# Attention and an expert layer on one core: the order of all operations laid out anew, with the filling matmuls placed again

## The chip, the core and the metric

The kernel runs on one core of one Trainium2 chip. The metric is device time in microseconds (us), median of the runs. A core has TensorE (PE: matmuls and transposes, with weight loads shown as PEld), VectorE (DVE), ScalarE (ACT), GpSimd (POOL) and SyncE (SP), each with its own queue of instructions that it works off in order. They wait for one another through semaphores.

## The reference, cut to what matters

Inputs are q, k and v of shape (4, 8, 768, 64): batches, heads, positions, width. A chunk is 32 positions of k; each query keeps the 6 chunks with the highest upper bound, and only those behind it.

```python
ub = sum(maximum(q * k_min, q * k_max), axis=-1)      # k_min, k_max per chunk of 32
ub = where(causal, ub, -1e9); top_chunks = argsort(ub)[..., -6:]
scores = where(chunk is in top_chunks and pos_q >= pos_k, q @ k.T / 8, -1e9)
attn = softmax(scores) @ v                             # (4, 8, 768, 64)
x = attn as (3072, 512)
h = x @ w_in                                           # (512, 2048)
out = softplus(h) @ w_out                              # (2048, 512)
```

## The kernel before

The work is cut into 12 blocks of 256 queries (4 batches of 3 blocks, all 8 heads at once as 4 pairs). For each block n the stages are:

- loads of q, k and v (`ld`), and transposes: blocks 0 to 2 on PE (`kT`, `qT`, L480), later ones by DMA from SP's queue (`kD`, `qD`);
- largest and smallest key of each chunk on DVE (`kx`, `kn`, L499 and L507), copies of these into a block-diagonal tile BD (`bd`), copies of K and of q into their places (`kc`, `qac`), positive and negative parts of q (`qpn`);
- the bounds on PE (`ub`, L579 and L583), on DVE the causal addition (`uba`), the sixth largest (`mx`, L606) and the mask (`raw`, L621 and L624, tile `mraw`), its transpose (`mT` on PE for blocks 0 to 2, L636 and L642; `mD` by DMA later) and the copies of the mask beside q (`mc`), so that the scores' matmul adds it;
- scores (`s`, L696 and L697, two matmuls each), exponential on ScalarE (`ex`, L704), the causal cut on GpSimd (`af`, L714), times v (`av`, L726), division on DVE (`nm`, L739 and L740), transpose into x (`oT` and `xc` in blocks 0 to 2 and 11, `xD` by DMA otherwise);
- the expert layer: `h` on PE (L895), exponential and logarithm on ScalarE (`e` L900, `ln` L905), the second matmul `y`. Blocks 4 to 10 make it of seven half-size products (L840) with differences on DVE (`dl`, `dh`, `dd`, `de`, `df`) and sums of the weights (`wd`, `wh`, `wv`); the others plainly (L925). The epilogue's small operations are `yr`, `yz`, `yv`, `yc`, `yd`, `ye`, `yw`, `yx`, `yf`, and `st` stores.

Nothing of this is in program order. `make_plan` makes operations with their dependencies, and the string `ORDER` lists all of them in one sequence: a letter for the engine (P, A, V, G, S), the name and, with #, which of that name (without #, the next one not yet placed). `in_order` hands out buffers in that sequence, and each engine's instructions are issued in it; a semaphore is all that holds an instruction back at run time. Many operations may run on either of two engines, and the letter chooses.

A word `z` with a number is no work of the plan: it makes matmuls on a tile of zeros, one of 512 columns (L1011) for every four and one of 128 columns (L1013) for each of the rest. They write a PSUM bank that the next real user clears.

```python
if word[0] == "z":
    order.append(int(word[1:]))
...
for _ in range(o // 4):
    nc.tensor.matmul(T.pools["y"].homes[0], T.zero, wide, start=True, stop=True)
for _ in range(o % 4):
    nc.tensor.matmul(T.pools["y"].homes[0][:, 0:128], T.zero, T.zero, start=True, stop=True)
```

Of the kernel before, what the change touches and what calls it, by code (L numbers as in the profile page):

```python
# [1047 lines left out]
```

## Time and profile before

| | |
|---|---|
| median of 3 runs | 256.06 us (256.02 to 256.46) |
| the profiled execution's own time | 256.22 us |
| its span, first to last instruction | 254.5 us |
| PE, ACT, DVE, POOL busy | 247.7, 212.2, 177.5, 119.6 us |
| matmuls | 2790, of them 86 on zeros |

The span is what the trace shows of one execution; what lies around it (256.22 less 254.5) is not seen in it. A matmul's row lasts longer than its place in the stream, as the next one starts before it ends: a PE that is shown busy can still have started its matmuls later than it could have. So the starts of matmuls are compared, beside the busy time.

### The profile page before, as it was taken

The page shows a single profiled execution, that of the slowest core. Times are in us where ns is not written, and L with a number is a line of the kernel's source. Part 1 is how long each engine was busy: PE and PEld are TensorE (multiplying, and loading weights), DVE is VectorE, ACT ScalarE, POOL GpSimd, SP SyncE. Part 2 cuts the span into 40 slices and gives each one's busy share as a digit, 9 for nine tenths or more (in the row PEclk, how much of TensorE's full clock was granted, in tenths as well). Part 3 has the DMA queues.
Part 4 walks back from the last instruction along what each step waited for, and adds up shares of the span by engine and source line. Part 5 has one row for each costly group of instructions (what it writes and reads, how often), then busy time and mean ns, then how long its engine had stood idle before and what let it go on. Part 6 is the DMA issues. An engine that isn't in the chain of part 4 may idle for free.

```text
span 254.5 us, 7076 instructions
## 1 busy us (share of the span) xinstructions
PE 247.7 (97%) x2790; PEld 202.7 (80%) x2790; DVE 177.5 (70%) x568; ACT 212.2 (83%) x389; POOL 119.6 (47%) x197
## 2 busy tenths in 40 slices
...
GB/s 170 147 133 129 193 195 193 162 164 152 138 130 145 188 157 135 142 172 194 159 146 158 100 119 168 43 24 36 8 85 62 3 206 3 1 85 3 0 58 193
DMA packets 113954, 29.90 MB, mean 117 GB/s; under 512 B 103776, under 2 KB 110944, under 8 KB 113920
## 3 DMA queue, kind: packets, MB, share of 16 engines
...
## 4 chain that ended last, share of the span: by engine, by line
PE 88%; DVE 8%; DMA 2%; issue 1%; ACT 0%; DVEq 0%
PE ph L895 31%; PE py L925 10%; PE pt L840 9%; PE py L840 8%; PE ps L696 6%; PE po L726 6%; PE ps L697 4%; PE py L1011 3%; DMA mT<-mraw 2%; PE ph L925 2%; PE pt L696 2%; DVE kx L507 2%; PE pt L726 2%; PE pt L579 2%; PE pt L697 1%; DVE qa L294 1%
## 5 line engine op out<-in xcount | busy, mean ns | idle before, releaser
L895 PE MATMUL ph<-x,w_in_sb 128*128 128x256 bf16 x768 | 97.9, 272 | 0.0
L704 ACT ACTIVATE pt<-ps 128x512 bf16<-128x512 f32 (+1 forms) x145 | 75.5, 550 | 9.3 <-PE ps L697 8.2
L714 POOL TENSOR_SCALAR_AFFINE_SELECT pt<-pt 128x256 bf16<-128x256 bf16 x96 | 40.7, 447 | 89.5 <-ACT pt L704 80.7
L895 PEld LDWEIGHTS <-w_in_sb 128*128 128x128 bf16 x768 | 72.4, 98 | 9.0
L900 ACT ACTIVATE e<-ph 128x512 f32<-128x512 f32 x96 | 57.0, 607 | 15.2 <-PE ph L895 15.0
L905 ACT ACTIVATE g<-e 128x1024 bf16<-128x1024 f32 x48 | 50.5, 1065 | 0.4
L925 PE MATMUL py<-w_out_sb,g 128*128 128x512 bf16 (+1 forms) x144 | 33.5, 367 | 0.0
L726 PEld LDWEIGHTS <-pt 128*128 128x128 bf16 x672 | 28.5, 97 | 2.6
L704 ACT ACTIVATE pt<-pt 128x512 bf16<-128x512 f32 (+1 forms) x47 | 26.3, 571 | 3.9 <-PE pt L697 3.1
L925 PEld LDWEIGHTS <-g 128*128 128x128 bf16 x176 | 16.4, 98 | 11.7
L726 PE MATMUL po<-v,pt 128*128 128x65 bf16 x516 | 24.4, 193 | 0.0
L840 PEld LDWEIGHTS <-g 128*128 128x128 bf16 x224 | 21.2, 98 | 2.6
L499 DVE TENSOR_REDUCE kx<-kT 128x32 bf16<-128x1024 bf16 x18 | 21.5, 1209 | 1.1 <-DMA kT<-io 1.0
L363 POOL DMA_DIRECT2D v<-in_v_dram x24 | 21.7, 908 | 0.0
L363 POOL DMA_DIRECT2D io<-in_k_dram x22 | 20.1, 921 | 0.0
L363 POOL DMA_DIRECT2D io<-in_q_dram x22 | 19.7, 901 | 0.1
L696 PE MATMUL ps<-qa,ka 96*128 96x256 bf16 x72 | 19.0, 273 | 0.7 <-DVE qa L294 0.6
L696 PE MATMUL ps<-qt,kb 128*128 128x256 bf16 x73 | 19.1, 272 | 0.0
L739 DVE RECIPROCAL rew<-po 128x4 f32<-128x4 f32 x38 | 6.7, 177 | 16.1 <-PE po L726 15.9
L840 PEld LDWEIGHTS <-df 128*128 128x128 bf16 x168 | 16.0, 98 | 2.0
L697 PE MATMUL ps<-qt,kb 128*128 128x256 bf16 (+1 forms) x73 | 17.3, 245 | 0.0
L740 DVE TENSOR_TENSOR osw<-po,rew 128x256 bf16<-128x256 f32 x38 | 16.1, 424 | 1.3
...
## 6 DMA issues: line engine op xcount, KB each, us to landing
out_dram<-ysb SPq DMA_DIRECT2D x23, 256.0 KB, 2.6
...
wx<-in_k_dram SPq DMA_DIRECT2D x2, 256.0 KB, 3.8
wx<-in_q_dram SPq DMA_DIRECT2D x2, 256.0 KB, 4.0
```

What stands on the lines that cost most here:

```text
L363: lambda e, t=t: nc.gpsimd.dma_start(out=into(nm, n, t), in_=rows(nm, n, t)),
L499: nc.vector.tensor_reduce(kx.ap[:, :, j].rearrange("d p (t c) -> d t p c", t=NT), kT.ap.rearrange("d p x -> d (p x)").rearrange("d (t p c ...
L696: nc.tensor.matmul(sp.ap[:, 0:QB], kk[0:nr, p, j * 128:(j + 1) * 128], qq, start=True, stop=True)
L697: nc.tensor.matmul(sp.ap[:, QB:w], kk[0:nr, p, (j + 1) * 128:(j + 2) * 128], qq[:, 1] if last else qq, start=True, stop=True)
L704: lambda e, sp=sp, pt=pt, h=h, j=j, w=w: nc.scalar.activation(pt.ap[:, h, j:j + 2].rearrange("k j c -> k (j c)")[:, 0:w], sp.ap[:, 0:w], A ...
L714: nc.gpsimd.affine_select(out=d, in_=d, compare_op=ALU.is_ge, fill=0.0, base=0, channel_multiplier=-1, pattern=[[0, 2], [1, 128]])
L726: nc.tensor.matmul(o[:, u, h], pt.ap[:, h, j, c0:c0 + 128], T.V[i][:, j, 2 * p + h, :], start=(j == 0), stop=(j == t0 + u))
L840: nc.tensor.matmul(bank.ap[:, c * HD:(c + 1) * HD], a(f), w(f), start=start and f == 0, stop=f == HF - 1, skip_group_check=True)
L895: nc.tensor.matmul(o[:, j], T.w_in[:, dt, ft * 128:(ft + 1) * 128], x.ap[:, dt], start=(dt == 0), stop=(dt == KDM - 1))
L900: lambda e, hb=hb, eb=eb, f2=f2: nc.scalar.activation(eb.ap[:, f2 * 512:(f2 + 1) * 512], hb.ap, ACT.Exp),
L905: lambda e, eb=eb, g=g, f4=f4: nc.scalar.activation(g.ap[:, f4 * 4:(f4 + 1) * 4].rearrange("f j c -> f (j c)"), eb.ap, ACT.Ln, bias=1.0),
L925: nc.tensor.matmul(yb.ap[:, 0:c1 - c0], g.ap[:, f, u * 128:(u + 1) * 128], T.w_out[:, f, c0:c1], start=(f == 0), stop=(f == KFF - 1))
```

## The change

`ORDER` is replaced by another sequence of the same operations; no other line changes. The real matmuls, transposes, loads and stores are the same. Three things differ.

- The sequence on each engine, from the first loads to the last stores.
- The engine of some operations. To DVE from ScalarE: the cast of q's first half of block 0, one K copy of block 0 (`kc0`), one `xc0`, one `xc11`, one `mc3`, one `ye0`, one `ye1`, `yd` of blocks 5, 6, 8, 9 and 10, and `ye4`, `yr5` and `yr8` with `yr4`. To ScalarE from DVE: two `mc0`, one `kc2`, one `qpn8`, `ye5`, `ye8`, `ye9`, `yr7`, `yr9`. Between GpSimd and DVE: `qac0` (one), `wd0`, `wd2`, one `wh0`, one `wh2`, `yw8`, `yw9`, `yx8` to DVE, and `wd4`, `yw5`, `yw6`, `yx10` to GpSimd.
- The zeros: 24 words with 53 wide and 33 narrow matmuls become 29 words with 46 wide and 37 narrow. All stand, as before, ahead of the first `h`.

The first lines of both sequences (to beyond the transpose of block 2's mask, `PmT2`) and the last ones:

```diff
@@ -199,84 +199,85 @@
 ORDER = """
-Vzero Sld_k0.0 Acast_k0.0 Vmr0#1 Vkb0 Vmr0 Gvone Gident z32 PkT0 PkT0 Sld_q0.0 Vr4 Gc4 Vbd0 Vkx0 Vkn0 Sld_k0.1
-Vcast_k0.1 Acast_q0.0 z6 PqT0 PqT0 Aqc0 Vbd0#2 Gld_k1.0 Gld_k1.1 Vqpn0 Aqpn0 Sld_q0.1 Acast_q0.1 z36 PqT0 Gld_q1.0
-Gld_q1.1 PkT1 Vcm0 Voh Akc0 Akc0 PkT0 PkT0 Sohk Sohk#3 Sohk PqT0 Vkx0 Vkn0 Aqc0 Aqpn0#3 z5 PkT1 Pub0 Gld_q2.0 Aqpn0
-Akc0#3 Vmx0 Vraw0 Gqac0#1 Gbd0#3 Gqac0 Gld_v0.0 Gld_v0.1 Vkx1 Sohk z28 PmT0 PqT1 PqT1 Amc0 Aqc1 Vkn1 Vbd1 Vkc1 z16
-Ps0#2 z5 Pub0 Ps0 Vmx0 Vqpn1 Vraw0 z35 PmT0 Vqac1 Amc0 Aqpn1 Pub1 Aex0#2 Aex0 Akc0 Vmc0#3 Gld_k2.0 Gld_k2.1 Vmc0 z7
-Ps0#4 Ps0 Aex0 Gld_q2.1 Gld_v1.0 Aex0#4 Gld_v1.1 Gaf0 z12 Ps0#5 Aex0#5 Vmx1 Vraw1 z3 Ps0 Gaf0 Aex0 Pav0 z3 Pav0 Gaf0
-Gw_in0 Vnm0 Gaf0 PqT2 Gw_in1 Gld_q3.0 Ps0#7 PmT1 Vmc1 Gw_in2 Akc1 z4 PoT0 Ps0 Aex0 Aex0 z12 Ps1#12 Pav0 Pav0 Aex1#12
-Axc0 PkT2 PkT2 Ps1#4 Vmc1 Gaf0#6 Gaf0 Gaf0 Aex1#4 Vnm0 Gaf0 Gld_k3.0 z3 PqT2 Ps1#5 Aex1#5 PoT0 z1 Ps1#7 z5 Ps1 Gcm z10
-Pav0#6 Pav0#7 Gvone Vkx2 Vkn2 Vnm0#3 Axc0 Aqc2 Aex1#7 Aex1 z7 Ps1 Aex1 z3 Pav0 Vbd2 Vqpn2 Vqpn2 Ps1#3 Aex1#3 Gaf1#1
-PoT0#3 z1 Ps1 z4 Ps1#15 Pav0 Vnm0 Vkc2 Vqac2 Aex1 Gaf1 z4 Ps1#8 Pub2 Axc0#3 Aex1#15 Ps1#11 Aex1#8 Aex1#11 Gw_in3 PoT0
-Ps1#13 Pav1 z3 Ps1#9 Pav1 Gld_k3.1 Aex1#13 Gw_out0 Gaf1#6 Gaf1 Ps1#14 Axc0 Vmx2 Gaf1#7 Vraw2 Aex1#9 Aex1#14 Ph0 Ps1#10
-Aex1#10 Ps1 Vnm1 Gaf1 Aex1 Ae0 Gaf1 Gld_q3.1 PmT2 Vmc2 Ph0 Gaf1 Pav1#6 Pav1#7 Vnm1#3 Vkc2 Ps2#6 Ae0 Gld_v2.0 Aex2#6
-Ps2#8 Aex2#8 Ph0#3 Aln0 Ps2#2 Pav1 Pav1 Ps2 Aex2 Ph0 SkD3 Vnm1 Vmc2 Ps2#12 Pav1 Pav1 Aex2#2 PoT1 Vxc1 Ae0 Vnm1 Ps2#5
-Vbd0 PoT1 Ph0 Aex2#12 Aex2#5 Ae0 Ps2#17 PoT1 Ps2#14 Aex2#17 Vxc1 Vxc1 Ph0 PoT1 Vxc1 Ps2 Aex2#14 Ae0 Ps2#9 Ae0 Aex2 Ph0
...
-Pav11#7 Aln10 Axc11 Aex11 Aln10#3 PoT11 Py9 Vnm11#3 Py9 Vyv9 Pav11 Pav11 Ph10 Ae10 Vxc11 Vnm11 Py9#12 PoT11#3 Py9 Py9
-Py9 Ae10 Axc11#3 Aln10 PoT11 Vxc11 Py9#13 Ph11#6 Ph11#7 Py9 Ae11#6 Ae11#7 Ph11 Vyc9 Vdl10 Vye9 Gyw9 Vdh10 Ayd9 Ae11
-Vyx9 Vdd10 Vdf10 Vde10 Ph11#4 Py10 Py10 Py10 Ph11 Ae11 Aln11 Py10#4 Py10#5 Py10#6 Ae11#4 Ph11#5 Ae11#5 Py10#7 Ph11
-Vyr10 Py10 Py10 Ph11 Ae11 Ae11 Sst8 Sst8 Vyz10 Py10#12 Aln11#3 Vyv10 Py10 Py11#8 Py10 Py11 Vyc10 Vyf9 Aln11 Py10#13
-Aln11 Py11 Py10 Py11 Py11 Aye10 Ayd10 Py11 Py11 Py11 Py11 Vyw10 Vyx10 Vyf10 Sst9 Sst10#1 Sst10 Sst9 Vye11 Sst11 Aye11
-Sst11 Py11 Py11 Py11 Aye11 Sst11
+Vzero Gident Sld_k0.0 Acast_k0.0 z32 PkT0 Vkb0 Sld_q0.0 Vcm0 Vmr0#1 Sld_k0.1 PkT0 Vcast_q0.0 z6 PqT0 Vbd0 Vr4 Vkx0 Gcm
+Gvone Sld_q0.1 Vkn0 Vcast_k0.1 Gld_q1.0 Gld_q1.1 z31 PkT0 Vmr0 Akc0#1 Gld_k1.0 Gld_k1.1 Acast_q0.1 PqT0 Aqc0 PkT0 PqT1
+Aqpn0 Aqpn0 z13 PqT1 Gld_q2.0 Vbd0#2 Gqac0 Voh Vkx0 Vkc0 Sohk Sohk z15 PkT1 PqT0 PqT0 Aqc1 Gc4 Aqc0 Vkn0 Akc0 Aqpn0 z1
+Pub0 Gbd0#3 Gld_v0.0 Vqac1 Vmx0 z2 PkT1 Gld_v0.1 Vqpn0 Vraw0 z11 PmT0 Pub0 Amc0 Amc0 z8 Ps0 z7 Ps0 Aex0 Aex0 Vkx1 Vmx0
+Sohk#3 Gld_q2.1 Vqpn1 Aqpn1 Vraw0 Vkn1 Vqac0 z5 Ps0 Aex0 Vbd1 Vbd0 Gld_k2.0 Vkc1#1 PmT0 Gaf0#1 z28 Pub1 Vmx1 Amc0 Amc0
+Ps0#6 Akc0 Gld_k2.1 z7 Ps0#7 Sohk Aex0#6 Aex0#7 Vraw1 Gld_v1.0 Gw_in0 Gaf0#2 Gaf0 z5 Ps0 Aex0 Pav0 Akc1 z2 Pav0 Ps0
+Aex0 Vnm0 Gaf0 z1 Ps0 PmT1 PqT2 z1 Pav0 PqT2 Pav0 Aex0 Vmc1 Aqc2 Vnm0 z8 Ps1#4 Gld_v1.1 Ps1#5 PkT2 Gaf0#6 Gaf0#7 z2
+Pav0#6 Pav0#7 PoT0 Gw_in1 Gw_in2 Vmc1 Gld_k3.0 Aex1#4 Aex1#5 z2 PkT2 Ps1 Gaf0#5 Gaf0 Aex1 Vqpn2 Gw_in3 Gaf1#2 Gld_k3.1
+Vnm0#3 z1 Ps1#12 z8 Ps1#13 Aex1#12 Aex1#13 Vxc0 Gld_q3.0 z4 Ps1#3 Aex1#3 PoT0#3 z1 Ps1#2 Aex1#2 z4 Ps1#7 z6 Ps1#6 Pav0
+Pav0 Aex1#7 Ps1#8 Axc0#3 Vkx2 Vkn2 Vbd2 PoT0 Aex1#6 z5 Ps1 Axc0 Aex1#8 Vqpn2 z1 Pub2 Ps1#10 Aex1 Gaf1 Gaf1 Aex1#10
+Vqac2 Vnm0 Ps1#15 PoT0 Vmx2 z4 Pav1 Pav1 Ps1#14 Aex1#15 Axc0 Ps1 Aex1#14 Aex1 Gld_q3.1 Vraw2 Ph0#1 Ps1 Akc2 Aex1 PmT2
+Gw_out0 Ph0 Ae0 Ae0 Vnm1 Gaf1#7 Gaf1#6 Gaf1#4 Vmc2 Pav1#6 Pav1#7 Gw_out1 Ps2#8 Ps2#6 Vkc2 Ph0 Aex2#6 SkD3 Vnm1#3
+Aex2#8 Gaf1 PoT1 Pav1 Ps2#12 Gaf1 Ae0 Ps2 Pav1 Vmc2 Aex2#12 Aex2 Vnm1 Vxc1 PoT1#3 Aln0 Ph0 Ps2#16 PoT1 Ps2#14 Pav1 Ph0
+Aex2#14 Aex2#16 Ps2#17 Pav1 Ae0 Aex2#17 Ps2#5 Vnm1 Vxc1 Aex2#5 Gaf2#4 Ae0 Ph0#6 Gld_v2.0 Gaf2#5 Gld_v2.1 Ps2#2 Ps2#11
...
+Py9#6 Py9#7 Pav11 Vyz9 Vyf8 Vnm11 Py9 Py9 PoT11#3 Vxc11#3 Py9 Py9#12 PoT11 Axc11 Aln10#3 Vyv9 Ph10 Py9 PoT11 Ae10 Ae10
+Aln10 Py9#13 Py9 Vxc11 Ph11 Ae11 Aye9 Vyd9 Vdl10 Vde10 Vdd10 Vyc9 Ph11#6 Py10 Py10 Sst8 Ae11#6 Ph11#4 Ae11#4 Ph11#5
+Ae11#5 Ph11#2 Ph11 Vdh10 Vyw9 Vyx9 Sst9#1 Ae11 Aln11 Ae11 Vdf10 Py10#4 Py10#5 Py10 Ph11 Py10 Vyr10 Vyz10 Ae11 Py11
+Ph11 Py10 Py10 Py10#12 Aln11 Aln11 Ae11 Aln11 Py11 Py10 Py10#13 Py10 Py11 Sst8 Vyf9 Aye10 Vyv10 Vyd10 Vyc10 Py11#4
+Py11#5 Py10 Py11#6 Py10 Vyw10 Gyx10 Vyf10 Sst10#1 Sst9 Sst10 Py11#7 Py11 Py11 Aye11 Vye11 Sst11#1 Sst11 Py11 Py11 Py11
+Aye11 Sst11
 """
```

## Rows read from the trace of the kernel before

**Rows 1.** The page: span, and busy time with share of the span.

```profile
span 254.5 us, 7076 instructions
...
PE 247.7 (97%) x2790; PEld 202.7 (80%) x2790; DVE 177.5 (70%) x568; ACT 212.2 (83%) x389; POOL 119.6 (47%) x197
```

**Rows 2.** Busy time by stretch: us, engines, granted PE clock, DMA share, GB/s.

```profile
20.00:30.00 10.00, 9.95 (x144) 7.73 (x141) 8.89 (x28) 9.68 (x21) 8.86 (x18) 1.00 1.18 159
...
200.00:210.00 10.00, 10.00 (x106) 8.99 (x104) 4.41 (x9) 9.90 (x20) 0.41 (x1) 1.00 0.43 133
```

**Rows 3.** Groups by line: count, busy us, mean ns, idle before.

```profile
L1011 PE MATMUL py<-zero 128*128 128x512 bf16 x53 | 15.9, 417 | 1.1 <-DVE zero L303 1.1
...
L294 DVE COPY qa<-qt 64x1024 bf16<-64x1024 bf16 x11 | 5.8, 530 | 0.0
...
L1013 PE MATMUL py<-zero 128*128 128x128 bf16 x33 | 4.3, 218 | 0.0
...
L294 DVE COPY x<-pt 128x256 bf16<-128x256 bf16 x8 | 2.2, 281 | 7.6 <-PE pt L757 7.6
```

**Rows 4.** The chain of waits in order of time: start, us, what.

```profile
22.66 0.45 PE pt L480 x8
...
45.94 0.86 PE py L925 x4
```

**Rows 5.** Timeline around 31 us: start, us, engine, instruction, [idle before, releaser].

```profile
30.71 1.84 POOL L714 TENSOR_SCALAR_AFFINE_SELECT pt<-pt 128x256 bf16<-128x256 bf16 x5
...
31.40 1.21 DVE L624 CAST mraw<-ub 128x16 bf16<-128x16 f32 x1
...
32.67 0.40 PE L642 MATMUL pt<-ident,mraw 128*128 128x128 bf16 x4 [0.78 <-DVE rew L739]
```

**Rows 6.** Timeline of the first 29 us, single rows of DVE, ACT and PE.

```profile
1.06 3.59 PE L1011 MATMUL py<-zero 128*128 128x512 bf16 x8 [1.06 <-DVE zero L303]
...
2.88 0.27 DVE L323 MEMSET mraw<- 128x256 uint32 x1
3.09 0.21 DVE L315 COPY rows<-ident 128x128 bf16<-128x128 bf16 x1
...
3.28 0.22 DVE L324 MEMSET bd<- 128x192 uint32 x1
...
4.70 0.62 ACT L293 CAST io<-wx 128x512 bf16<-128x512 f32 x1 [0.22 <-DMA wx<-in_q_dram]
...
5.17 1.29 DVE L507 TENSOR_REDUCE kx<-ph 128x16 bf16<-128x512 bf16 x2 [1.67 <-PE ph L480]
...
6.40 0.90 DVE L294 CAST io<-wx 128x512 bf16<-128x512 f32 x1
...
7.64 0.57 ACT L293 COPY ka<-ph 64x512 bf16<-64x512 bf16 x1
...
10.84 0.17 DVE L624 CAST mraw<-ub 128x8 bf16<-128x8 f32 x1
...
16.11 0.62 DVE L624 CAST mraw<-ub 128x8 bf16<-128x8 f32 x1
...
17.30 0.42 DVE L294 COPY qt<-ph 32x512 bf16<-32x512 bf16 x1 [0.33 <-PE ph L636]
...
27.92 0.18 DVE L739 RECIPROCAL rew<-po 128x4 f32<-128x4 f32 x1 [0.55 <-PE po L726]
...
28.48 0.67 DVE L294 COPY ka<-pt 64x1024 bf16<-64x1024 bf16 x1
```

**Rows 7.** Timeline around 106 and 122 us, PE's rows at the two gaps.

```profile
105.52 0.46 PE L726 MATMUL pt<-v,pt 128*128 128x65 bf16 x10
...
106.20 0.27 PE L696 MATMUL ps<-qa,ka 96*128 96x256 bf16 x1 [0.21 <-DVE qa L294]
...
119.78 1.89 PE L925 MATMUL py<-w_out_sb,g 128*128 128x512 bf16 x8
...
122.08 0.27 PE L696 MATMUL ps<-qa,ka 96*128 96x256 bf16 x1 [0.40 <-DVE qa L294]
```

More of the change, by code (lines that the diff above doesn't have):

```diff
@@ L277 @@
[L277 to L279 removed]
+Vzero Gident Sld_k0.0 Acast_k0.0 z32 PkT0 Vkb0 Sld_q0.0 Vcm0 Vmr0#1 Sld_k0.1 PkT0 Vcast_q0.0 z6 PqT0 Vbd0 Vr4 Vkx0 Gcm
+Gvone Sld_q0.1 Vkn0 Vcast_k0.1 Gld_q1.0 Gld_q1.1 z31 PkT0 Vmr0 Akc0#1 Gld_k1.0 Gld_k1.1 Acast_q0.1 PqT0 Aqc0 PkT0 PqT1
@@ new lines @@
+Vwv0 Sst3 Sst0 SkD10 Py3 Ps7#8 Vdd4 Ae5 Aex7#7 Aex7#13 Ps7#11 Aex7#8 Sst2 SmD9 SxD6 Py3 Ps7 Ps7#9 Py4 Ph5 Py4 Aex7#11
+Aex7#9 Gaf7#2 Vdh4 Vkx8 Gaf7#4 Vkn8 Vkc8#1 Gaf7#6 Gld_v7.1 Gaf7#1 Gld_k11.0 Gaf7#7 Gaf7#3 Gld_v9.0 Aye3 Gaf7 Aex7
+Ps7#14 Aex7#14 Ps7#10 Ps7 Py4#4 Py4#5 Py4 Py4#6 Py4#7 Aln5 Aln5#2 Ae5 Aex7 Ph6 Ae6 Ph5#6 Pav7#2 Vmc9#1 Amc9 Aex7 Vyr4
+Vyz4 Vdf4 Py4 Pav7#3 Ph6 Pav7 Ps9#1 Pav7 SqD8 Ae5#6 Vkx10 Ps9 Aex9 Py4#12 Aqpn8 Py4 Py4 Vqpn8 Vqac8 Ps9#4 Py4#13 Vkn10
+Gaf9 Gld_v9.1 Ae6 Aex9 Vbd8 Vkc8 Vnm7 Vyv4 Vyc4 Gaf7 Gld_v10.0 Gaf9 Vye4 Vnm7 Gld_k11.1 Ph5 Ae5 Aln5 Py4 Pav7#6
@@ new lines @@
+Gld_v8.1 Pav7#7 Pub8 Ayd4 Ph5 Ps9#6 Aex9#4 Py4 Ae5 Aex9#6 Vuba8 Vyw4 Ph6#6 Ae6#6 Ph6#7 Ae6#7 Aln5 Ps9#7 Vmx8 Vkc10
+Vraw8 Vnm7#3 Gyx4 Ps9 Vyf4 Pav7 Ps9 Pav7 Ph6#3 Aex9 Aex9#7 Vdl5 Vde5 Aln6 Ph6 Py5 Ae6 SmD8 Ps9 Py5 Py5#4 Aex9 Ae6
+Gaf9#7 Gaf9#4 Aex9 Gaf9#5 Gaf9#3 Py5#5 Pav9 Gaf9#6 Pav9 Ph6#5 Ph6 Vnm7 Vmc8 Vmc8 Ps8 Vdd5 Vyr5 Vdh5 Vnm9 Sst3 SxD7
+Sst2 SqD10 Pav9#4 Pav9#5 Py5#6 Py5#7 Ps8#3 Aln6#3 Ae6 Aex8 Py5#8 Aln6 Aex8#3 Vkc10 Vdf5 Ps8#2 Ps8#4 Py5 Aex8#4 Ae6 Ph7
+Ps8#5 Vnm9#2 Gaf9 Aex8#5 Vyz5 Pav9 Py5#9 Py5 Ps8#12 Py5#12 Ps8#13 Pav9 Aex8#2 Ae7 Aex8#12 Aln6 Vyv5 Vqpn10 Vqpn10
@@ new lines @@
+Py5#13 Py5 Aex8#13 Vnm9 Ph7#2 Ps8#14 Vbd10 Vqac10 Vyc5 Ps8#23 Ps8#18 Py5 Aye5 Aex8#14 Ps8#6 Pav9 Pav9 Py6 Py6 Vdl6
+Vyd5 Vdh6 Ae7#2 Aex8#6 Ps8#21 Gyw5 Vyx5 Vde6 Vyf5 Vnm9 SkD11 Vkx11 Aex8#18 Aex8#23 Aex8#21 Ph7 Ps8#17 Ps8#10 Aex8#10
+Ph7#4 Ps8#8 Aex8#8 Py6#4 Py6#5 Pub10 Ps8#7 Ae7 Aex8#17 Ayr6 Ae7#4 Aex8#7 Ph7 Ps8#20 Vdd6 Py6 Py6#6 Vuba10 Vmx10 Vraw10
+Ps8#19 Sst5#1 Sst4 Py6 Ph7#6 Ps8 Ae7 Sst4 Aln7 Aex8#20 Py6 Ps8#15 Aex8 Py6 Py6 Aex8#19 Ps8 SxD9 SmD10 Gld_q11.0
+Gld_q11.1 Aex8#15 Ae7#6 Aln7 Gaf8#6 Vyz6 Vkn11 Vdf6 Vbd11 Ph7#7 Gaf8#5 Gaf8#7 Gld_v11.0 Ps8#22 Ps8 Vkc11 Gld_v10.1
@@ new lines @@
+Vyv6 Py6#12 Py6#13 Gaf8#1 Gaf8#2 Gaf8 Pav8 Pav8 Vyd6 Ph9#4 Aex8#22 Aex8#11 Gaf8 Vyc6 Vye6 Vkc11 Pav8#6 Vnm8 Ae7#7
+Aln7#3 Aex8 Ph9#5 Vmc10 Ae9#4 Ps8 Ps10 Aex10 Aex8 Vmc10 Py6 Py6 Gyw6 Vyx6 Ps10 Ps10#3 Pav8#7 Gaf8 Vnm8#3 Aex10 Vdl7
+Pav8#4 Pav8#5 Ae9#5 Ph7 Aex10#3 Ae7 Aln7 Py7 Py7 Pav8 Vyf6 Vnm8#2 Pav8 Ps10#12 Aex10#12 Vnm8 Vde7 Ps10#8 Py7 Py7
+Ps10#4 SqD11 Vdh7 Vqpn11 Aex10#8 Py7 Ps10#9 Py7 Ps10#11 Vdd7 Aex10#4 Aex10#9 Ayr7 Vyz7 Vqpn11 Vdf7 Ps10#7 Ps10#13
+Aex10#11 Ph9 Ps10#6 Ph9 Sst6 SxD8 Aex10#13 Aex10#7 Aex10#6 Pub11 Ps10#5 Ae9 Ae9 Aex10#5 Gaf10#6 Gaf10#4 Ph8#2 Ae8#2
@@ new lines @@
+Aln8#3 Sst7 Sst6 Ps11#5 Py8 Aex11#5 Ph9#6 Aex11#11 Ae8 Vdl8 Ae9#6 Gaf11#3 Ps11#7 Py8 Ps11#2 Py8 Ph9#7 Aex11#22 Aex11#7
+Aex11#2 Gaf11#5 Gaf11#2 Ps11#19 Ph9 Ae9#7 Ps11#23 Ps11#9 Ph10#6 Aln8 Aex11#23 Ps11#21 Ps11 Aex11#9 Ae9 Aex11#21
+Ps11#16 Pav11#2 Aex11#19 Gaf11#7 Ph10#7 Aex11#16 Ae10#6 Ae10#7 Ps11 Aex11#3 Vde8 Vdd8 Py8 Py8 Vdh8 Vdf8 Vyr8 Vyz8
+Gaf11#6 Gaf11 Gaf11#4 Gaf11 Aln9#3 Aex11 Ps11#13 Pav11#3 Ph10#1 Ps11 Aex11 Py8 Py8 Vyv8 Vyc8 Aex11 Ph10 Ae10 Aln9 Py8
+Pav11 Py8 Py8#12 Pav11 Vnm11 Ae10 Py8 Ps11 Py8 Ph10#5 Ph10#4 PoT11 Py8 Ae10#4 Vdl9 Vdh9 Vnm11 Vdd9 Vde9 Aye8 Vyw8
```

128 lines of the change are left out of this document (51 added, 77 removed).

## The prediction

> **What bounds the kernel now.** I read the page first. TensorE (PE) is busy 97% of the span, so the question is only how much of PE's time is useful [rows 1]. The table of busy times by stretch then splits the kernel: a stretch late in the kernel is full (10.00 of 10), and so is 20 to 30 us (9.95 of 10), but that early stretch is partly filled with matmuls on zeros [rows 2]. The groups by line give their number: 53 of 512 columns and 33 of 128 columns [rows 3]. Their pace when nothing holds PE is taken from the chain of waits: four 512-column matmuls in 0.86 us are 0.215 us each, eight 128-column ones in 0.45 us are 0.056 us each [rows 4]. So zeros cost 53 x 0.215 + 33 x 0.056 = 13.2 us.
>
> I counted the matmuls of the two orders from their lists. Ahead of the transpose of block 2's mask (L642, `mT2`) both place exactly the same real work, about 12.0 us at full pace, and all their zeros. In the trace that transpose starts at 32.67, after PE sat 0.78 us idle [rows 5]. Behind it PE has the same real matmuls to do in either order, and almost no gaps. The time is therefore: the start of `mT2`, plus a fixed sum, plus the gaps behind it, plus a tail. The tail is the same: both lists end with three groups of 256-column matmuls, a ScalarE copy and one store.
>
> In the front 33 us VectorE (DVE) sets the pace. Its first reduction starts at 5.17 and ends a 1.67 us wait; after that only two waits of note are left, 0.33 before a mask copy and 0.55 before a reciprocal [rows 6]. The last DVE step before `mT2` is a cast that took 1.21 us beside GpSimd's five selections, where the same kind of cast of half the width took 0.17 in one place and 0.62 in another [rows 5, 6].
>
> Behind the front I found two gaps worth naming. Ten 65-column matmuls start at 105.52; at the pace of about 0.03 us each they are issued by 105.82, but the next matmul starts at 106.20: 0.38 us lost to the first scores of block 6, which wait for DVE's mask copy. Eight 512-column matmuls start at 119.78, are issued by 121.50 (8 x 0.215), and the next starts at 122.08: 0.58 us for block 7 [rows 7]. (The 0.03 is an estimate: the ten took 0.46 in their row, of which the last one's own length, about 0.2, is no pace.)
>
> **Terms.**
>
> *Zeros.* The new list has 46 wide and 37 narrow ones: 7 x 0.215 - 4 x 0.056 = 1.28 us less work on PE. 1.14 of it lies between the bounds of block 1 (`ub1`) and of block 2 (`ub2`): 14 wide and 23 narrow become 10 and 18, that is 4.30 to 3.16. There PE was full, so zeros may themselves have delayed what stood behind them: the gain lies between 0 and 1.14, depending on whether DVE and ScalarE deliver sooner.
>
> *DVE's front chain.* What is added between the landing of q's first half and `mT2`: the cast of q0 (0.90, by the cast that DVE does now), the clearing of BD (0.22), the copy for rows4 (0.21), the clearing of Mraw (0.27), one K copy from PSUM (0.57, by ScalarE's), one copy of q (at most 0.53, the mean of such copies of twice the width; GpSimd did it before), one x copy (0.28), and the second clearing of BD (0.22): 3.20 us [rows 3, 6]. The clearings were free before because DVE was waiting for data anyway; in the new list they stand behind the cast of q0. Taken away: two mask copies of block 0 (2 x 0.42) and one K copy of block 2 (0.67): 1.51 [rows 6]. Net +1.69. DVE can begin 0.47 us sooner, since the cast of q0 needs only data that ScalarE's cast had at 4.70, against 5.17: +1.22. That is the upper end. From it come off up to 0.88 us of waits (0.33 + 0.55) and up to 1.04 of the slow cast (1.21 to 0.17) [rows 5, 6], as GpSimd's selections no longer stand beside it: the lower end is -0.70. The new list has two DMA issues of GpSimd next to that cast, so I take its 0.62 form, 0.59 off, and half the waits: 1.22 - 0.59 - 0.44 = +0.19.
>
> The rows show that one kind of cast took 0.17, 0.62 and 1.21 us, the last beside five selections of GpSimd [rows 5, 6]. The Trainium skill, SBUF — State Buffer, section "Who interferes with whom", says that VectorE's copies and casts in a two-port mode and GpSimd share one pair of ports, held for a whole instruction, so that the loser waits it out; this speaks against moving copies to VectorE in the front, and by it the six moved or added small operations could each wait for a GpSimd issue, which would give the upper end, +1.22, not +0.19.
>
> *ScalarE in the front.* It gets two copies of block 0's mask and one K copy of block 2, and loses a cast, a K copy of block 0 and an x copy. Up to the first expert matmul that is three jobs less for two more, all of about 0.6 us like the cast and the K copy of the rows, or shorter [rows 6]: no loss, and I price it at nothing. The K copy of block 2 comes after that matmul, whose PE time covers it; uncovered it is about 1 us (twice the width of the 0.57 one), a price like that of the slow rivals.
>
> *The front together.* Two views: DVE's sum says +0.19; PE's zeros say up to -1.14. The stretch from `ub1` to `ub2` has both engines near full, so I take a value between, -0.4, and keep -1.3 and +1.2 as ends.
>
> *The two gaps.* On PE the work between block 6's bounds and its first scores grows from 8.0 to 10.5 us (counted from the lists with the paces above): the 0.38 goes. For block 7 it stays at 9.2, with the DVE work between changed in order only: I take half, -0.29 of 0.58. For blocks 5, 8 and 11 this cover shrinks (9.2 to 8.2, 11.7 to 10.1, 11.8 to 8.8), so I add 0.3 for a new gap; bounds 0 and 1.4 (new waits as deep as the two deepest seen, 0.78 + 0.58). The other moves (weight sums between GpSimd and DVE, epilogue copies between ScalarE and DVE) lie beside a full PE and are priced at nothing; were their cover gone, each is one copy of about 0.4 us.
>
> Sum: -0.4 - 0.38 - 0.29 + 0.3 = -0.77. The profiled execution took 256.22 us, so 255.45; the runs' median stands 0.16 below it: **255.3 us**.
>
> **Rivals.** (1) *Nothing comes of it.* DVE's sum holds (+0.2), one of two gaps goes, one of the same size appears: 256.0. For it: DVE's list is longer; against: less zero work.
> (2) *More comes of it.* Zeros were in the way (-1.14 to -1.3), both gaps go (-0.96) and none appears: 256.06 - 2.2 = 253.9. For it: 20 to 30 us is full with zeros in it; against: zeros elsewhere end in waits.
> (3) *DVE is late, slower than before.* The late start of the key reductions, about 6.0 (4.70 + 0.90 + 0.22 + 0.21) against 5.17, is never caught up: the mask of block 0's first pairs comes after 13, and `mT2` at 33.9: +1.2, with the gaps half mended -0.3: 257.0. It decides from the point where `mT2` starts later than 33.3.
> (4) *A new wait behind the front*, at block 5's, 8's or 11's first scores: +1.4 - 0.4 (front) - 0.4 (block 6): 256.06 + 0.6 = 256.7.
> (5) *The clock.* PE's granted clock is full in all rows here. The first eight zero matmuls take 3.59 us, 0.43 each [rows 6], twice their later pace. If the thinner zeros near 10 to 17 us brought that pace back for a while, the roughly 2 us of real work there would take 1 us more on the way to `mT2`: 257.0. Nothing in the trace shows it after the start.
>
> **Chances.** Forecast 0.37, (1) 0.20, (2) 0.20, (3) 0.13, (4) 0.06, (5) 0.04. The forecast's own range is 254.8 to 255.8. One measurement can tell about 0.2% (0.5 us) from no change, so faster means below 255.55. Faster: 0.20 + 0.28 of the forecast's 0.37 = 0.48. Same: 0.09 + 0.20 + 0.01 = 0.30. Slower: 0.13 + 0.05 + 0.04 = 0.22. The range reaches from (2) to (3): 253.9 to 257.0, leaving out under 0.1 on each side.
>
> **What would show it.** Zeros 46 and 37 in the groups by line; `mT2`'s start (L642) at about 32.3, before 31.4 for (2), after 33.3 for (3); the first DVE reduction at about 6.0; the cast before `mT2` at 0.6 instead of 1.21; no idle PE before L696 between 95 and 125. The forecast is wrong if DVE's front is full and later than before, or if PE shows idle time anywhere between 35 and 250 us that is longer than the two gaps were.

## The result

The kernel became slower: 260.39 us (258.53 to 261.32, 6 runs) against 256.28 us before in the same measurement, a ratio of 1.0147 with an interval of 1.0103 to 1.019. The prediction was 255.3 us. In this document a ratio leaves out executions more than 1.5% above the fastest of their kernel, while medians and ranges count all. The profiled execution took 261.32 us, the longest of the six, with a span of 259.6; its page and its table by stretch, where the page's counts answer to [rows 1] and the first and last rows of the table to [rows 2] (columns: PE, PEld, DVE, ACT, POOL busy, granted PE clock, DMA share, GB/s):

```profile
span 259.6 us, 7066 instructions
...
PE 248.5 (96%) x2772; PEld 203.4 (78%) x2787; DVE 183.1 (71%) x580; ACT 210.2 (81%) x381; POOL 117.0 (45%) x193
```

```profile
20.00:30.00 10.00, 9.36 (x132) 7.20 (x131) 9.46 (x31) 8.85 (x19) 9.56 (x16) 1.00 1.27 169
...
90.00:91.00 1.00, 0.00 (x0) 0.00 (x0) 0.99 (x2) 0.00 (x0) 1.00 (x2) 1.00 2.06 140
91.00:92.00 1.00, 0.30 (x3) 0.27 (x3) 0.95 (x3) 0.00 (x0) 1.00 (x2) 0.95 1.32 84
92.00:93.00 1.00, 0.98 (x5) 0.68 (x5) 0.93 (x3) 0.83 (x2) 0.99 (x2) 0.50 1.83 127
93.00:94.00 1.00, 0.80 (x2) 0.30 (x2) 0.97 (x4) 1.00 (x3) 1.00 (x2) 0.50 1.62 142
94.00:95.00 1.00, 1.00 (x5) 0.55 (x4) 0.91 (x3) 0.23 (x1) 1.00 (x2) 0.50 1.58 192
95.00:96.00 1.00, 1.00 (x10) 0.82 (x9) 0.99 (x3) 0.60 (x1) 1.00 (x2) 0.85 2.43 157
200.00:210.00 10.00, 10.00 (x117) 9.04 (x116) 4.40 (x14) 9.87 (x19) 0.15 (x1) 1.00 0.35 107
```

The zeros came out as counted, 46 wide and 37 narrow ones, and the front is faster: the last DVE cast ahead of `mT2` (L625 here, L624 in [rows 5]) at 0.21 us instead of 1.21, and `mT2` at 31.62 with no idle time ahead of it, 1.05 us earlier than before. Groups of the two zero lines, then single rows of the timeline:

```profile
L1012 PE MATMUL py<-zero x46: 376/379/635, 1.1 to 29.4; 128*128 128x512 bf16 x46
L1014 PE MATMUL py<-zero x37: 217/219/314, 5.5 to 27.4; 128*128 128x128 bf16 x37
```

```profile
4.80 0.43 DVE L295 CAST io<-wx 128x512 bf16<-128x512 f32 x1 [1.92 <-DMA wx<-in_q_dram]
...
5.50 1.28 DVE L508 TENSOR_REDUCE kx<-ph 128x16 bf16<-128x512 bf16 x2
...
31.10 0.21 DVE L625 CAST mraw<-ub 128x16 bf16<-128x16 f32 x1
...
31.62 0.39 PE L643 MATMUL pt<-ident,mraw 128*128 128x128 bf16 x4
```

The loss is behind that. PE's rows with waits, in the timeline of the changed kernel:

```profile
77.42 0.27 PE L697 MATMUL pt<-qa,ka 96*128 96x256 bf16 x1 [0.72 <-DVE qa L295]
...
91.70 0.27 PE L697 MATMUL ps<-qa,ka 96*128 96x256 bf16 x1 [2.10 <-DVE qa L295]
91.81 0.32 PE L698 MATMUL ps<-qa,ka 96*128 96x256 bf16 x1
91.92 0.42 PE L697 MATMUL pt<-qa,ka 96*128 96x256 bf16 x1
...
114.56 0.18 PE L580 MATMUL pt<-bd,qpos 128*128 128x32 bf16 x1 [0.58 <-DVE osw L741]
...
145.92 0.60 PE L841 MATMUL py<-wx,df 128*128 128x256 bf16 x4 [0.35 <-DVE ysb L856]
```

They are the first scores of block 4 (77.42) and of block 5 (91.70), the bounds of block 7 (114.56) and a product of block 4 (145.92). Where the text gives a wait, it counts, as in the prediction, from where the matmuls ahead are issued at their usual pace, some 0.16 us more than the idle time in a row's brackets. Behind 91.70 the same 256-column matmul stretches from 0.27 to 0.42 us, and the granted clock in the table is 0.50 for three microseconds, the lower of its two levels (1.2 GHz), after PE had done nothing for 2.1 us. I set the two traces side by side at equal amounts of PE's real work. The difference (after less before) is -1.0 us at 40 us, about 0 behind block 4's wait (+0.95), +3.7 behind block 5's wait and the slow stretch, +4.1 from 146 us to PE's last matmul (the gaps of [rows 7] gone: -0.35 and -0.55; the waits at 114.56 and 145.92: +0.7 and +0.5), and +5.1 at the end of the span: the last 0.95 us is in the stores behind the last matmul. (This is the balance of the longest execution; the medians differ by 4.1 us.)

Block 5's wait in the chain of waits, and what DVE and GpSimd did then in the timeline:

```profile
82.36 1.51 DVE ub L607 x16
...
84.78 5.10 DMA mT<-mraw
...
89.94 1.06 issue
90.99 0.66 DVE qa L295
...
91.70 0.27 PE ps L697
```

```profile
89.90 1.75 DVE L295 COPY qa<-mT 32x512 bf16<-32x512 bf16 x2 [1.48 <-DMA mT<-mraw]
...
87.78 1.12 POOL L364 DMA_DIRECT2D v<-in_v_dram  x1
88.90 0.88 POOL L364 DMA_DIRECT2D io<-in_q_dram  x1
89.76 0.89 POOL L364 DMA_DIRECT2D io<-in_k_dram  x1
90.63 0.90 POOL L364 DMA_DIRECT2D v<-in_v_dram  x1
```

Before the change, SP's and DVE's rows, and the landing of this one transpose (lowest, median and highest are the same):

```profile
83.14 1.20 SPq L645 DMA_TRANSPOSE mT<-mraw  x1
...
87.86 1.28 DVE L294 COPY qa<-mT 32x512 bf16<-32x512 bf16 x2
...
DMA to landing us min/median/max: 3.8/3.8/3.8
```

The mask is ready at 84.75. Its transpose by DMA (`mD5`) takes 5.10 us from issue to landing, where before the change it took 3.81 (issued 83.14), and the two copies behind it take 1.75 us while GpSimd issues loads without a pause (1.28 before, with loads beside most of it). Before, the copies started 0.9 us after the landing, because DVE was still at other work; now DVE waits for the landing. In SP's list two stores (`st1`) now stand ahead of `mD5`; before, one did.

### The profile page after: what moved, and what is told of

It is laid out like the page before. It is cut to its first block, busy times and chain, and to the rows that moved or that the text cites. A ratio compares the mean times of both kernels' runs of the same rounds, so it can differ in the third digit from the quotient of the medians.

```text
span 259.6 us, 7066 instructions
## 1 busy us (share of the span) xinstructions
PE 248.5 (96%) x2772; PEld 203.4 (78%) x2787; DVE 183.1 (71%) x580; ACT 210.2 (81%) x381; POOL 117.0 (45%) x193
## 4 chain that ended last, share of the span: by engine, by line
PE 78%; DVE 11%; DMA 4%; ACT 3%; issue 2%; DVEq 0%
PE ph L896 28%; PE py L926 9%; PE py L841 8%; PE pt L841 7%; PE ps L697 5%; PE po L727 4%; PE ps L698 4%; PE py L1012 2%; DMA qt<-io 2%; DMA mT<-mraw 2%; PE ph L926 2%; PE pt L697 2%; PE pt L727 2%; PE pt L580 2%; PE pt L698 2%
## 5 line engine op out<-in xcount | busy, mean ns | idle before, releaser
L705 ACT ACTIVATE pt<-ps 128x384 bf16<-128x384 f32 (+1 forms) x146 | 76.7, 556 | 9.5 <-PE ps L698 8.8
L896 PEld LDWEIGHTS <-w_in_sb 128*128 128x128 bf16 x768 | 73.2, 98 | 9.9
L715 POOL TENSOR_SCALAR_AFFINE_SELECT pt<-pt 128x256 bf16<-128x256 bf16 x96 | 41.4, 455 | 81.2 <-ACT pt L705 76.9
L926 PE MATMUL py<-w_out_sb,g 128*128 128x512 bf16 (+1 forms) x131 | 32.4, 372 | 0.9 <-issue 0.2
L705 ACT ACTIVATE pt<-pt 128x512 bf16<-128x512 f32 (+1 forms) x46 | 25.6, 564 | 4.3 <-PE pt L698 4.0
L926 PEld LDWEIGHTS <-g 128*128 128x128 bf16 x176 | 16.4, 99 | 11.6 <-issue 0.6
L727 PE MATMUL po<-v,pt 128*128 128x65 bf16 x452 | 22.1, 193 | 0.0
L364 POOL DMA_DIRECT2D io<-in_q_dram x22 | 20.4, 928 | 0.1
L698 PE MATMUL ps<-qt,kb 128*128 128x128 bf16 (+1 forms) x74 | 17.6, 244 | 0.0
L698 PE MATMUL ps<-qa,ka 96*128 96x128 bf16 (+1 forms) x72 | 17.3, 246 | 0.0
L856 POOL TENSOR_TENSOR ysb<-ysb,ysb 128x256 f32<-128x256 f32 x2 | 1.4, 724 | 33.8 <-DVE ysb L856 33.8
```

The source lines that it names most:

```text
L364: lambda e, t=t: nc.gpsimd.dma_start(out=into(nm, n, t), in_=rows(nm, n, t)),
L698: nc.tensor.matmul(sp.ap[:, QB:w], kk[0:nr, p, (j + 1) * 128:(j + 2) * 128], qq[:, 1] if last else qq, start=True, stop=True)
L705: lambda e, sp=sp, pt=pt, h=h, j=j, w=w: nc.scalar.activation(pt.ap[:, h, j:j + 2].rearrange("k j c -> k (j c)")[:, 0:w], sp.ap[:, 0:w], A ...
L715: nc.gpsimd.affine_select(out=d, in_=d, compare_op=ALU.is_ge, fill=0.0, base=0, channel_multiplier=-1, pattern=[[0, 2], [1, 128]])
L727: nc.tensor.matmul(o[:, u, h], pt.ap[:, h, j, c0:c0 + 128], T.V[i][:, j, 2 * p + h, :], start=(j == 0), stop=(j == t0 + u))
L896: nc.tensor.matmul(o[:, j], T.w_in[:, dt, ft * 128:(ft + 1) * 128], x.ap[:, dt], start=(dt == 0), stop=(dt == KDM - 1))
```

## The experiments

Each edit is in the list of operations, unless code is shown. Ratios are to the kernel before in the same measurement, with their intervals.

**Halves.** h1: new order up to `mT2`, old order behind; h2: the reverse.

> The new order up to the transpose of block 2's mask (mT2), then every other operation in the old order and on its old engine. Theory W (the loss is behind the front, at block 5's first scores and the stores at the end): mT2 starts near 31.6 as in the new kernel, the rest as before, so about 1.0 us less than the kernel before: 255.2 us. Rival F (the thinner zeros or the new front upset what comes later): slower than the kernel before, 257 us or more, with idle PE behind 80 us.

> The old order up to mT2, then the new one. Theory W: the wait before block 5's first scores stays (PE idle about 2 us near 91, granted clock at half for some 3 us), and the front's 1.0 us are lost too: 261 us. Rival F: the loss goes with the front, 256 to 257 us.

h2 took 259.14 us, 1.0107 (1.0049 to 1.0166), between the two theories: `mT2` at 32.33 and the waits of blocks 4 (0.89), 5 (2.33), at 114 (0.74) and at 146 (1.0) all there, so they belong to the new rest. Its profiled execution had block 5's wait with a full granted clock behind it. h1 took 258.04, 1.0067 (1.004 to 1.0094), rival F's time but not its place: `mT2` 1.36 us earlier, but then the old rest met two loads that had not landed:

```profile
48.36 1.02 PE L944 MATMUL py<-w_out_sb,g 128*128 128x512 bf16 x4 [1.32 <-DMA w_out_sb<-in_moe_w_out_dram]
...
51.84 0.34 PE L745 MATMUL po<-v,pt 128*128 128x65 bf16 x6 [1.04 <-DMA v<-in_v_dram]
```

**Block 5: the clock.** e3 fills the wait with ten zero matmuls:

```
 def f_s(...):
+    if (n, p, h, j) == (5, 1, 0, 0):
+        for _ in range(10): nc.tensor.matmul(sp.ap, T.zero, <zeros, 512 columns>, start=True, stop=True)
```

> The new order with ten 512-column matmuls on zeros ahead of the first scores of block 5, into the bank that these write next, so that PE works while it waits there (10 x 0.215 = 2.15 of the 2.26 us). Theory W with the clock as a result of that idle PE: the scores start when they did, the granted clock stays full between 90 and 100 us, and about 1.5 us come back: 258.9 us. Rival C (the clock falls by itself or by other gaps): half clock still shows, and the time stays at 260.4 us.

258.51 us, 1.008 (1.0052 to 1.0108). The scores start as late as in the changed kernel (2.28 us), but the clock stays full:

```profile
89.00:92.00 3.00, 3.00 (x20) 1.60 (x18) 2.43 (x4) 0.75 (x2) 2.99 (x5) 1.00 1.86 133
92.00:93.00 1.00, 0.94 (x7) 0.48 (x6) 0.93 (x4) 1.00 (x3) 1.00 (x1) 1.00 2.28 147
```

What block 5 costs is +2.2 us with the zeros and +3.8 without: 1.6 us is the clock. All five executions of e3 have a mean clock of 0.998 or more, against 0.993 in four of the changed kernel's six.

**Block 5: the wait.** e4 moves work into it, `Py2#3 Ph3#4` ahead of `Ps5#6`.

> The new order with one y step of block 2 and one h step of block 3 (1.73 us of PE work) moved ahead of the first three scores of block 5. Theory W: the wait shrinks from 2.26 to about 0.5 us, the clock stays full, 1.73 + 1.5 us come back: 257.2 us. Rival: PE runs out of ready work at the next step instead and nothing is gained, 260.4 us.

259.14 us, 1.0101 (1.0067 to 1.0134): the wait splits into 0.53 (`s5#6`), 0.91 (`s5#18`, which waits for a division that stands behind the second mask copy on DVE), and 0.33 us (`s5#22`, which waits for ScalarE). Of the 3.2 us that I expected back, about 1.3 came. The next three go at the causes:

```
e5:  - Sst1#0 Sst1#1 SmD5        + SmD5 Sst1#0 Sst1#1
e6:  + last["ld v8.0"].gate.append(last["mc5"])      (GpSimd's loads wait for the mask copies)
e7:  both
```

> The changed order with one move: on SP, block 5's mask transpose mD5 is issued ahead of block 1's two stores st1#0 and st1#1 instead of behind them. Theory A (the transpose lands late because it stands behind two stores): its 5.10 us from issue to landing fall to the 3.8 us it took before the change or less, s5#6 starts about 1.3 us earlier, the 2.26 us wait shrinks to about 1.0, TensorE's granted clock stays at full behind it, and the time falls by 1.3 (wait) to 2.9 us (wait and clock): 257.5 to 259.1 us against 260.4 for the changed kernel. Theory B (what delays it is the loads that GpSimd issues meanwhile, not the stores): it still takes about 5 us, s5#6 starts within 0.3 us of where it did, time 260 to 260.7.

> The changed order, with GpSimd's load issues from v8.0 on made to wait for block 5's second mask copy mc5#1. Theory A (the first mask copy mc5#0 takes 1.75 us because GpSimd's load issues run beside it): it falls to 0.7 to 0.9 us, s5#6 starts 0.8 to 1.0 us earlier, the wait falls from 2.26 to about 1.3 us; 259.4 if TensorE's clock still falls behind it, about 257.8 if it no longer does. Theory B (the copy is long for another reason, its input's landing for one): it stays at 1.5 us or more and the time stays at 260 to 260.7. The later loads cost up to 0.5 us further on in either case.

> Both edits at once: mD5 ahead of the stores, and the loads from v8.0 on behind mc5#1. If block 5's wait has the two causes that I give it, they add: s5#6 starts 2.1 to 2.3 us earlier, the wait is 0 to 0.3 us, the granted clock stays full between 92 and 96 us, and the time is 260.4 - 3.8 = 256.6 us, with 256.0 to 257.3 as the range because the other waits (block 4's 0.9, block 6's 0.7) stay. If the transposes and copies are late for another reason the time stays above 258.5.

e5 took 257.9 us, 1.0096 (1.0066 to 1.0126), in the range of theory A. The transpose takes 3.47 us, `s5#6` starts with no wait, and the clock stays at 1.00. Over all 18 profiles `mD5` took 3.5 to 4.3 us with no `st1` store ahead of it (e5, e7, e8), 3.8 to 4.9 with one (ten profiles) and 4.9 to 5.7 with two (five). So 5.10 against 3.81 compares with the shortest of the ten; the mean of those is 4.5. Single rows of e5's timeline, DVE's mask copies and PE's scores:

```profile
88.61 0.83 DVE L312 COPY qa<-mT 32x512 bf16<-32x512 bf16 x2
89.48 1.74 DVE L312 COPY qt<-mT 32x512 bf16<-32x512 bf16 x2
...
89.59 0.27 PE L714 MATMUL ps<-qa,ka 96*128 96x256 bf16 x1
...
91.94 0.27 PE L714 MATMUL pt<-qa,ka 96*128 96x256 bf16 x1 [0.67 <-DVE osw L758]
```

The copies beside the loads are still slow: it is the second one now, 1.74 us. It ends at 91.22, the division behind it on DVE (`osw`) ends at 91.89, and `s5#18`, which by the profile waits for that division, starts at 91.94, 0.83 us late. e6 shows the other cause: the transpose stays at 5.09, and both copies take 0.58 us.

```profile
85.04 5.09 DMA mT<-mraw
```

```profile
90.16 0.58 DVE L312 COPY qa<-mT 32x512 bf16<-32x512 bf16 x2 [1.47 <-DMA mT<-mraw]
90.77 0.58 DVE L312 COPY qt<-mT 32x512 bf16<-32x512 bf16 x2
...
107.16 0.38 PE L745 MATMUL po<-v,pt 128*128 128x65 bf16 x7 [1.26 <-DMA v<-in_v_dram]
```

Theory A holds at the place (the wait is 1.09 us, the clock full) and fails in the time, 260.31 us, 1.018 (1.0132 to 1.0229): the loads that were held back are late at 107.16. e7 has both effects, block 5's wait is down to 0.19 us, and still took 258.96 us, 1.0128 (1.0075 to 1.0181), with 1.2 us lost to the same late load and 1.4 to another at 50.15.

**The other waits.** e8 is e5 with four moves: `Vkc4#1` behind `Vmc4#0` and `Pav3#7` ahead of `Ps4#12`; `Ph3#4` ahead of `Ps5#18`; `Ps6#6 Ps6#5 Py3#0` ahead of `Pub7`; `Vyv4` ahead of `Vkx10`.

> The changed order with mD5 ahead of the stores (as in e5) and four small moves, one for each wait that e5 still had: the second key copy of block 4, kc4#1, behind mc4#0 and av3#7 ahead of s4#12 (wait of 0.90 us); h3#4 ahead of s5#18 (0.83); s6#6, s6#5 and y3#0 ahead of ub7 (0.91); yv4 ahead of kx10 on VectorE (1.02). Theory A (the changed order loses by these waits alone, each caused by an operation placed before its input can be there, and what the front, block 6 and block 7 gained is real): the waits at 77, 92, 112 and 144 us shrink by 2.5 to 3.6 us in sum and nothing takes their place; against e5's 257.9 that gives 254.3 to 255.4, at or below the kernel before (255.7 to 256.3). Theory B (the work between is so tight that a wait removed comes back at the next operation): less than half of it reaches the end, 256.5 to 257.7.

259.23 us, 1.0127 (1.0094 to 1.016): slower than both theories had it. What theory B says is seen on PE: the waits at 112 and 144 are gone and the one at 77 is down to 0.30, but 0.58 us is left at block 5's first scores, which had none in e5, 0.6 appears at 95 and 1.57 at block 4's expert matmuls, which wait for `xD4`, a transpose that stands in SP's queue behind `kD7` and `mD6`. The chain of waits, then the timeline:

```profile
99.74 8.06 DMA x<-osw
```

```profile
107.85 0.39 PE L913 MATMUL ph<-x,w_in_sb 128*128 128x256 bf16 x2 [1.41 <-DMA x<-osw]
```

That is not what makes it slower than e5, though: in the two profiles PE's last matmul starts at 252.82 (e8) and 253.06 (e5), and the time from its end to the end of the span is 4.6 against 3.1 us.

**The front: zeros or cast.** z1 is the kernel before with six wide zeros fewer (1.28 us) between `ub1` and `ub2`. z2 is the kernel before with one gate, so that raw2's cast runs beside fewer selections: `af1[7].gate.append(raw2)`.

> The kernel before with nothing changed but the zeros between ub1 and ub2: six wide ones (24 columns' blocks of the count, 1.28 us) fewer. Theory A (the start of mT2 is set by VectorE, and zeros only fill TensorE's time ahead of it): mT2 starts within 0.3 us of 32.67 us, the idle time ahead of it grows from 0.9 to about 2 us, and the time stays at 256.0 to 256.5 us; so the front's gain in the changed kernel is VectorE's order, not the zeros. Theory B (the zeros themselves hold the front up): mT2 starts 0.7 to 1.3 us earlier and the time falls to 255.0 to 255.6 us. Theory C (fewer zeros let TensorE's granted clock fall): the clock is 0.5 in some stretch between 20 and 45 us, and the time rises by 1 us or more.

> The kernel before with one edit: GpSimd's selection af1#7 (and with it the ones queued behind) waits until VectorE has finished raw2, so that raw2's last cast runs beside no selection but the one already under way. Theory A (the front's gain is this cast: 1.21 us beside five selections, 0.21 in the changed kernel): the cast takes 0.2 to 0.6 us, mT2 starts at 31.7 to 32.1 us instead of 32.67, and, since the loads are issued where they were, 0.6 to 0.9 us reach the end: 0.25 to 0.35% faster than the kernel before. Theory B (what held mT2 is VectorE's whole list, or the gain is lost to a later wait as with the new front): mT2 at 32.4 or later, or a new wait of 0.6 us or more behind it, and no change in time within 0.2%.

z1: 257.27 us, 1.0011 (0.9984 to 1.0038). `mT2` starts at 32.68 against 32.67, behind the same slow cast. z2: the cast takes 0.19, and `mT2` follows without a wait. Timeline of z1, then of z2. (z2's execution is 1.25 us early before the gate acts: block 0's second mask transpose starts at 15.53 instead of 16.78, as three DVE operations ahead of it, the same in both kernels, took 0.42, 0.36 and 0.57 us instead of 0.90, 0.81 and 0.89.)

```profile
32.68 0.40 PE L661 MATMUL pt<-ident,mraw 128*128 128x128 bf16 x4 [0.78 <-DVE rew L758]
...
31.41 1.22 DVE L643 CAST mraw<-ub 128x16 bf16<-128x16 f32 x1
```

```profile
30.15 0.19 DVE L643 CAST mraw<-ub 128x16 bf16<-128x16 f32 x1
...
30.48 0.39 PE L661 MATMUL pt<-ident,mraw 128*128 128x128 bf16 x4
```

So one edit gives nearly the whole gain of the front: without those 1.25 us `mT2` is 0.95 us earlier, and it stays so to the end of that execution, the shortest of z2's twelve. The time doesn't show it: 256.42 us (253.82 to 259.35), 0.9997 (0.9962 to 1.0032). Theory A holds for the start of `mT2`, theory B for the time.

**Keeping the front's gain.** Six kernels tried. h1b is h1 with `w_out1` behind `w_out0` and `v2.1` behind `v2.0`; h1c and h1d change from the new to the old order at block 3's first scores and at `y1#0`; z3 is z2 with `Py2#7` ahead of `Ps6#2` and `Vdl4` behind `Vmc7#0` (the two gaps of [rows 7]); z4 is z2 with `w_out1`, `v2.0`, `v2.1` ahead of `q3.1`; z5 is z4 with z3's moves.

> The new order up to mT2, the old order behind it (as in h1_new_front_old_rest), with two load issues moved: w_out1 right behind w_out0, and v2.1 right behind v2.0. h1 lost 2.7 us in two waits, at 48.36 us for w_out1 and at 51.84 us for v2.1. Theory A (those loads stood too far back in the line of loads, and nothing else changes): w_out1 lands at about 43.6 and v2.1 at about 48.8 us as in the changed kernel, both waits go, and the 1.36 us that the front gained reach the end: 256.25 - 1.36 + 0.3 = 255.2 us, range 254.8 to 255.7. Theory B (the line of loads is full and something else is late next): one of the waits stays, 256 to 257.5.

> The new order up to block 3's first scores (s3#4, at about 56 us) and the old order for everything behind it. Theory A (all that the change lost lies behind 70 us, in the waits of blocks 4, 5, 6 and at 146 us, and all that it gained in the front reaches the end where the old order follows): TensorE is 0.8 to 1.3 us ahead at 56 us, the old order's gaps at 106 and 122 us (0.35 and 0.57 in the changed kernel's balance) close as the earlier start gives VectorE and the transfers more room, and the time is 255.7 - 0.8 = 254.9 us, with 254.0 to 255.3 as the range. Theory B (loads that came earlier or later than the old order needs them give it back, as in h1 and h1b): a wait of 1 us or more between 56 and 90 us, and 256 to 258.

> As h1c, with the seam one operation earlier, ahead of s3#4: in h1c that operation stood ahead of the old order's s3#2, held one of the score banks until ex3#4, and s3#6 waited 0.74 us for it. Theory A (the new front's gain reaches the end when nothing at the seam takes it): TensorE is 1.4 to 1.7 us ahead of the kernel before at 70 us and stays so, the profiled span is 252.7 to 253.2 us, and the median 254.6 to 255.4 us, below both kernels. Theory B (the transfers and loads, not TensorE, set the times from 56 us on, so that an earlier start meets them unlanded): new waits between 56 and 125 us, and a median of 255.8 to 257.

> z2 with two moves more: y2#7 ahead of s6#2 (the gap of 0.38 us at 106.2) and VectorE's subtraction dl4 behind mc7#0 (the gap of 0.57 us at 122.1). Theory A (a gap in front of a block's first scores is worth its length when the operation ahead of it is moved): both gaps are gone, and the time is 0.6 to 0.95 us below z2's, 0.5 to 0.7% below the kernel before, the fastest of all. Theory B (the wait reappears at the next operation, as in e8): 0.3 us or less below z2.

> z2 with three load issues of GpSimd in another order: w_out1 where q3.1 was, v2.1 right behind v2.0, q3.1 behind both. Theory A (in many executions the front's gain is lost at y0#1 and av2#1 to w_out1 and v2.1, whose landing lies close to their use): w_out1 lands about 2.5 us and v2.1 about 3.5 us earlier than in the kernel before, no wait stands at y0 or av2, and the median is 0.6 to 1.0 us below the kernel before. Theory B (the spread comes from elsewhere: the transfers of blocks 4 to 8, the last stores): the median stays within 0.3 us of z2's.

> z4 with z3's two moves (y2#7 ahead of s6#2, dl4 behind mc7#0). Theory A (each gap is worth its length): 0.6 to 0.95 us below z4. Theory B: within 0.3 us of z4, the wait comes back at the next operation or the spread hides it.

| kernel | us (lowest to highest) | ratio, interval | waits in its profile |
|---|---|---|---|
| h1b | 258.39 (255.42 to 260.24) | 1.0057 (1.0023 to 1.0091) | 1.35 for `v2.0` at 45.44 |
| h1c | 256.56 (255.37 to 259.89) | 1.0013 (0.9979 to 1.0046) | 0.74 at 65.26, a score bank |
| h1d | 257.39 (255.47 to 261.49) | 1.0018 (0.9995 to 1.0042) | 0.74 at 67.47, 0.96 at 90.28 |
| z3 | 256.22 (254.54 to 260.89) | 0.9993 (0.9966 to 1.002) | profile of its slowest execution: 0.98 and 1.81 for `w_out1` and `v2.1`, 1.79 at 132.34 |
| z4 | 260.71 (259.44 to 264.13) | 1.0185 (1.0147 to 1.0223) | 1.39 for `v2.0` at 45.81, 2.52 at block 3's bounds |
| z5 | 260.85 (259.94 to 263.92) | 1.0198 (1.0157 to 1.0238) | 0.77 and 2.76 at the same places |

None is clearly below the kernel before, though h1b, h1c and z2 each had a profile that ended 0.7 to 2.5 us earlier than [rows 1], each of one of its kernel's three fastest executions. h1b, h1c and h1d fall to theory B, and z4 is slower than both of its theories had it. z3 against z2 and z5 against z4 differ by 0.2 us or less, theory B, although the two gaps are gone in both profiles. z4 was a bad move: `q3.1`, put behind the three other loads, was issued at 35.62 instead of 32.50 and landed at 46.95 instead of 39.97, its transpose at 54.79, and block 3's bounds waited for it:

```profile
55.30 0.18 PE L598 MATMUL pt<-bd,qpos 128*128 128x16 bf16 x1 [2.36 <-DVE qpos L579]
```

## Why the prediction was wrong

*The frame* (start of `mT2`, fixed work, gaps, tail) was right: the balance above uses it and closes.

*The zeros.* Count right. That they might themselves delay `mT2` by up to 1.14 us: no, z1 shows 0.0.

*The front, -0.4.* Right in sign, -1.05 in fact, within the ends. The mis-sized term is the cast: 0.59 taken off, 1.0 measured, and z2 shows that it alone carries nearly all of the gain. The sign was luck: DVE's sum alone said +0.19, and -0.4 leaned on up to -1.14 for the zeros, which z1 found to be worth nothing in the old order. The upper end, every moved copy held up by a GpSimd instruction, did not come: the moved cast of q0 took 0.43 us, less than the 0.90 I took, and the first reduction began at 5.50, not 6.0. The rule of the Trainium skill that I cited for it (SBUF — State Buffer, "Who interferes with whom") agrees with 1.75 against 0.58 us for the same two copies in the changed kernel and e6, and with 1.22 against 0.19 for the same cast in z1 and z2. Which copies meet a GpSimd instruction, and lose time by it, was what I could not read from the lists: the cast that took 0.90 before took 0.42 in z2's profile, both times while GpSimd issued loads.

*The two gaps, -0.38 and -0.29.* -0.35 and -0.55: both went, block 7's wholly where I had taken half.

*"0.3 for a new gap", bounds 0 and 1.4: this is the step that failed.* It measured +0.95 (block 4), +3.8 (block 5), +0.7 (block 7's bounds) and +0.5 (the product at 146): 6.0 us. Three things were wrong in it. I counted as cover only the PE work between a block's bounds and its scores, and not how long the mask takes over the same distance. For block 5, bounds at 81.22 to scores at 91.70 is 10.5 us, where before it was 79.78 to 89.19, 9.4; the cover fell by 1.0 as I had counted, and the mask's way grew by 1.1: +1.3 with a store more ahead of its transpose on SP (5.10 against 3.81), +0.5 for load issues beside its copies (1.75 against 1.28), +0.2 up to the issue, and -0.9 because the copies no longer stood behind other work of DVE. e5 and e6 show the first two apart. Of the three blocks whose cover shrank only block 5 waited; at 8 and 11 no gap came. I had compared the lists of PE and DVE and not SP's. Second, block 4, whose cover is the same in both, was not in the list; there DVE had `nm3#2` and `kc4#0` between the mask and its copies, which stood elsewhere before, and only `qac4` less. Third, a wait had no price but its length, and block 5's cost another 1.6 us of clock (e3).

*"The tail is the same."* Not in that execution: 4.0 us from PE's last matmul to the end against 3.1. With the same last operations it was equal to before in the profiles of h2, e3, e5, e6 and e7, and 1.1 to 1.5 longer in e4 and e8; the last store took 2.29 us to land in the changed kernel's profile, 2.71 in e4's and 3.14 in e8's, and 1.67 before. What makes it slow is open.

*The rivals.* (4) had mechanism and place right, block 5's first scores, and its price wrong: 256.7 against 260.4. (5) had the kind right and the place wrong: the clock fell, not in the thinner zeros of the front, where it is 1.00 throughout, but behind the wait that (4) made.

Open: why z2's gain of 0.95 us, whole in its profile, is not in the median. The profile of z3's slowest execution has z2's gain at `mT2` and then loses 2.8 us at the two loads that h1 met. Up to block 6 the two kernels are the same, yet from issue to landing `w_out1` took 11.0 and `v2.1` 11.6 us there, against 7.9 and 6.2 in z2's profile. So I take the loads' landing for the reason; with one profile of each it is not shown for the median, and z4's attempt to move them made `q3.1` late and proves nothing about that.
